# First batch of an attention and feed-forward kernel: row sums as products with ones, division at the outputs, one filler product per bank

## The chip, the cores and the metric

One core of a Trainium2 chip runs the whole program. The metric is the device time of one execution in microseconds. The engines are TensorE (PE; its weight loads are listed as PEld), VectorE (DVE), ScalarE (ACT), GpSimd (POOL) and SyncE (SP), which issues the transfers.

## The reference

For 4 batches x 8 heads, 576 positions and a head dimension of 64:

```python
scores = q @ k.T / sqrt(64) + (cum[:, None] - cum[None, :])   # cum = cumsum(log(clip(f, 1e-4, 1)))
scores = where(causal, -1e9, scores) - max                    # causal: the part above the diagonal
attn = exp(scores); attn = attn / (sum(attn, -1) + 1e-9)
x = attn @ v                                  # heads side by side: 2304 tokens x 512
x = maximum(x @ w1, x @ w2, x @ w3) @ w_out   # 512 -> 768 -> 512
h = x @ w_in                                  # 512 -> 2048
out = ((a0 + a1*h + a2*h**2 + a3*h**3) / (1 + |b0|*|h| + |b1|*h**2 + 1e-6)) @ w_out2
```

The weights of both feed-forward layers arrive as 64-bit floats.

## The kernel before

Heads are worked on in pairs, and the 576 query rows in two groups: group 0 has the first 320 rows (three blocks), group 1 the last 256 (two blocks). The first batch goes through group 0 of its four pairs and then through group 1 of them, so that it makes up the first eight entries of the list of pairs (n from 0 to 7, one group each). Later batches have one entry for each pair with both groups. A unit is one head of one entry; a step takes a new unit through `scores`, the unit before it through `turn`, and the one before that through `attend`.

- `scores` makes the products of queries and keys in a PSUM bank (line 343 in 32-bit floats for the first six entries, lines 345 and 346 in two rounded parts afterwards). VectorE adds the mask and takes the row maximum (line 347), ScalarE takes the exponential and, through `accum_out`, the row sum (line 353).
- `normalise` adds 1e-9 to the row sums (line 358), takes their reciprocals (line 359), on VectorE, and lets GpSimd scale each block of exponentials by its row's reciprocal (line 362).
- `turn` transposes the blocks on TensorE (line 382), and ScalarE copies them into the tile `pt` (line 384).
- `attend`, once for both heads of a pair, multiplies `pt` by the values (line 398). In the result, `ot`, the partitions are the head's dimensions and the columns the queries. ScalarE copies it out as the rounded part of `x` (line 405), and VectorE subtracts for the rest (line 406).

PSUM has two banks for scores, three for transposes (`ps_t`, tag `t`), one for outputs (`ps_o`) and two for the first feed-forward layer. In the first four entries `exercised` puts filler products of 512 columns into each bank that is taken, ahead of the bank's real product, `WARM` of them (line 84); nothing reads their results.

Beside the attention run, call by call (`fill`), the conversions of the 64-bit weights (`convert`, lines 169 to 179: ScalarE, four VectorE instructions, ScalarE, then GpSimd) and the products of the first feed-forward layer (`moe1_h`, `moe1_o`, lines 430 to 461), whose intermediate maxima lie in three buffers with the tag `mx`. A planner puts the instructions of each engine in order by costs and due times of its own, save where the order is pinned; the outputs' products have high priority and are pinned among themselves. The second feed-forward layer follows, written out by hand from line 766 on.

Of the kernel before, what the change touches and what calls it, by code (L numbers as in the profile page):

```python
# [8 lines left out]
F32 = mybir.dt.float32  # L9
F32R = mybir.dt.float32r  # L10
I32 = mybir.dt.int32
AF = mybir.ActivationFunctionType
ALU = mybir.AluOpType
# [12 lines left out]
GBLK = [(0, 1, 2), (3, 4)]  # L26
# [11 lines left out]
def kernel(  # L38
    ctx: ExitStack, tc: tile.TileContext, q, k, v, f, w1, w2, w3, w_out, m2_in, m2_out, m2_a, m2_b, out
):  # L40
    nc = tc.nc
    B, H, S, D = q.shape
# [3 lines left out]
    P = 128  # L46
# [3 lines left out]
    NPAIR = H // 2  # L50
    NB = len(Q0)

    def r32(ap):
        return ap.bitcast(F32)
# [5 lines left out]
    const = ctx.enter_context(tc.tile_pool(name="const", bufs=1, side="left"))  # L60
    dram = ctx.enter_context(tc.tile_pool(name="dram", bufs=1, space=DRAM))
    mpool = ctx.enter_context(tc.tile_pool(name="mpool", bufs=1, side="left"))
    wpool = ctx.enter_context(tc.tile_pool(name="wpool", bufs=1, side="left"))
    apool_cm = ExitStack()
    apool = apool_cm.enter_context(tc.tile_pool(name="apool", bufs=1, side="right"))
    ps_cm = ExitStack()
    ps_s = ps_cm.enter_context(tc.tile_pool(name="ps_s", bufs=2, space=PSUM))
    ps_t = ps_cm.enter_context(tc.tile_pool(name="ps_t", bufs=3, space=PSUM))
# [11 lines left out]
    def exercised(bank, n):  # L80

        if n < 4:
            for _ in range(WARM):
                nc.tensor.matmul(bank, warm[:, 0], wide, start=True, stop=True)
        return bank

    WARM = 2
    mask = const.tile([P, S], F32, name="mask")
    nc.gpsimd.memset(mask, 0.0)
    nc.gpsimd.affine_select(  # L90
# [1 line left out]
        fill=-1.0e9, base=0, channel_multiplier=1,  # L92
    )


    NR = B * H
    fl = apool.tile([NR, S], F32, name="fl", tag="vs", bufs=3)
# [15 lines left out]


    LOOK, WHOLE, PRE = 2, 6, 2
    CONV2, EARLY = (32, 0.25), 12
    kqs = {}

    def k_split(i):
        if ("k", i) not in kqs:  # L120
            k1 = apool.tile([P, S], F32R, name=f"k1s{i}", tag=f"k1_{i}")
            kqs["k", i] = k1, apool.tile([D + 2, S], F32R, name=f"k2s{i}", tag=f"k2_{i}")
        return kqs["k", i]

    def q_split(g, i):
        if (g, i) not in kqs:
            w = GQ[g][1] - GQ[g][0]
            q1 = apool.tile([P, w], F32R, name=f"q1s{g}{i}", tag=f"q1_{g}_{i}")
            q2 = apool.tile([D + 2, w], F32R, name=f"q2s{g}{i}", tag=f"q2_{g}_{i}")
            nc.vector.tensor_scalar(q2[D : D + 2], mask[0:2, :w], 0.0, 1.0, op0=ALU.mult, op1=ALU.add)  # L130
            kqs[g, i] = q1, q2
        return kqs[g, i]
# [10 lines left out]
    for g in range(2):  # L143
        pts.append(apool.tile([P, 2, GCOLS[g]], F32, name=f"pt{g}", tag=f"pt{g}"))
        col = GCH[g][0][0]
# [81 lines left out]
    def pinned(ld):  # L227
        tc.keep_in_program_order(ld)
# [10 lines left out]
    SIDES = [(slice(0, D), slice(D, P)), (slice(D, P), slice(0, D))]  # L239

    class Pair:


        def __init__(self, n, b, hp, groups):
            self.n, self.b, self.hp, self.groups = n, b, hp, groups
            self.ng = groups[-1] + 1
            self.nk = GBLK[groups[-1]][-1] + 1
            self.ik = [(2 * n + h) % NKB for h in range(2)]
            self.iq = [[(2 * n + h) % m for h in range(2)] for m in NQB]
            self.pt = {}  # L250
            self.whole = n < WHOLE
            self.iqf = [(2 * n + h) % 4 for h in range(2)]

        def load(self):
# [58 lines left out]
    class Unit:  # L313
# [5 lines left out]

        def begin(self):  # L320
            self.st = apool.tile([P, 9], F32, name=f"st_{self.nm}", tag="st", bufs=3)
            self.rs = apool.tile([P, 2, 3], F32, name=f"rs_{self.nm}", tag="rs", bufs=3)

        def scores(self, i):
            p, h, g = self.pair, self.h, self.g
            if not p.whole:
                (k1, k2), (q1, q2) = k_split(p.ik[h]), q_split(g, p.iq[g][h])
            nr = P
            qs = slice(Q0[i] - GQ[g][0], Q0[i] - GQ[g][0] + P)
            keys = Q1[i]  # L330
            self.e[i] = apool.tile([P, keys], F32, name=f"e{i}_{self.nm}", tag=f"e{i}_{h}")
            e = self.e[i]
            st = self.st
            n0 = 3 * (i - GBLK[self.g][0])
            nm = st[:nr, n0 : n0 + 2]
            l = self.rs[:nr, 0, i - GBLK[self.g][0] : i - GBLK[self.g][0] + 1]
            parts = [(0, keys)] if keys <= 512 else [(0, 320), (320, keys)]
            off = S - P - Q0[i]
            for n, (a, z) in enumerate(parts):
                sp = exercised(ps_s.tile([P, 512], F32, name=f"s{i}_{n}_{self.nm}", tag="s"), p.n)  # L340
                if p.whole:
                    kf, qf = kfs[p.ik[h]][: D + 2], qfs[p.iqf[h]][: D + 2]
                    nc.tensor.matmul(sp[:nr, : z - a], qf[:, qs], kf[:, a:z], start=True, stop=True)
                else:
                    nc.tensor.matmul(sp[:nr, : z - a], q1[:, qs], k1[:, a:z], start=True, stop=False)
                    nc.tensor.matmul(sp[:nr, : z - a], q2[:, qs], k2[:, a:z], start=False, stop=True)  # L346
                nc.vector.tensor_tensor_reduce(  # L347
                    out=e[:nr, a:z], in0=sp[:nr, : z - a], in1=mask[:nr, off + a : off + z],
                    scale=-1.0, scalar=3.0e38 if n == 0 else nm[:, 0:1],
                    op0=ALU.add, op1=ALU.min, accum_out=nm[:, n : n + 1],  # L350
                )
            m = nm[:, len(parts) - 1 : len(parts)]
            nc.scalar.activation(e[:nr], e[:nr], AF.Exp, bias=m, scale=-1.0, accum_out=l)  # L353

        def normalise(self):
            blks = GBLK[self.g]
            n = len(blks)
            nc.vector.tensor_scalar_add(self.rs[:, 0, :n], self.rs[:, 0, :n], 1.0e-9)
            nc.vector.reciprocal(self.rs[:, 1, :n], self.rs[:, 0, :n])  # L359
            for j, i in enumerate(blks):  # L360
                e = self.e[i]
                nc.gpsimd.tensor_scalar(e, e, self.rs[:, 1, j : j + 1], 0.0, op0=ALU.mult, op1=ALU.add)  # L362
# [23 lines left out]
        def attend(self):  # L386

            p, h, g = self.pair, self.h, self.g
            if h == 0:
                return  # L390
            lo, hi = GQ[g]
            w = hi - lo
            ot = exercised(ps_o.tile([P, 512], F32, name=f"o_{self.nm}", tag="o"), p.n)
            order = list(GCH[g].items())
            with tc.high_priority():
                for j, (c, (col, q0)) in enumerate(order):
                    for i in (1, 0):
                        mm = nc.tensor.matmul(  # L398
                            ot[SIDES[i][0], q0 - lo : w], p.v[:, c, i], p.pt[g][:, i, col : col + hi - q0],
                            start=(j == 0), stop=(j == len(order) - 1),  # L400
                        )
                        if (j, i) != (0, 1):
                            pinned(mm)
            x = mpool.tile([P, 2, w], F32R, name=f"x_{self.nm}", tag=f"x{g}", bufs=(6, 8)[g])
            nc.scalar.activation(x[:, 0], ot[:, :w], AF.Copy)
            nc.vector.tensor_tensor(x[:, 1], ot[:, :w], r32(x[:, 0]), op=ALU.subtract)
            xt[p.b, p.hp, g] = x


    hs = {}  # L410
# [128 lines left out]
    for step in range(len(slots) + 2):  # L539
        u = slots[step] if step < len(slots) else None  # L540
        t = slots[step - 1] if 0 <= step - 1 < len(slots) else None
        o = slots[step - 2] if 0 <= step - 2 < len(slots) else None
        prep, NPRE = [], 0
        if u is not None and u.pair.n + 1 < len(pairs):
            n = u.pair.n + 1
# [252 lines left out]
```

## Time and profile before

| | |
|---|---|
| time, median of 3 runs | 966.98 us (966.38 to 970.47) |
| the profiled execution | 970.9 us, with a span of 969.1 us |
| busy, of the span | PE 97%, PEld 86%, DVE 76%, ACT 64%, POOL 26% |
| granted TensorE clock, mean | 0.988 |

The span reaches from the first instruction to the last. Busy shares are means over stages with different limits, so the rows below give them by stage. TensorE's matmuls are pipelined, and their ends are modelled: a busy TensorE is not one at its peak. A granted clock of 1.00 is 2.4 GHz, 0.50 is 1.2 GHz. "Idle before" is the time in which an engine waited just before an instruction, with what ended the wait.

### The profile page before, as it was taken

The page shows a single profiled execution, that of the slowest core. Times are in us where ns is not written, and L with a number is a line of the kernel's source. Part 1 is how long each engine was busy: PE and PEld are TensorE (multiplying, and loading weights), DVE is VectorE, ACT ScalarE, POOL GpSimd, SP SyncE. Part 2 cuts the span into 40 slices and gives each one's busy share as a digit, 9 for nine tenths or more (in the row PEclk, how much of TensorE's full clock was granted, in tenths as well). Part 3 has the DMA queues.
Part 4 walks back from the last instruction along what each step waited for, and adds up shares of the span by engine and source line. Part 5 has one row for each costly group of instructions (what it writes and reads, how often), then busy time and mean ns, then how long its engine had stood idle before and what let it go on. Part 6 is the DMA issues. An engine that isn't in the chain of part 4 may idle for free.

```text
span 969.1 us, 16846 instructions
## 1 busy us (share of the span) xinstructions
PE 943.1 (97%) x5780; PEld 829.9 (86%) x5780; DVE 739.6 (76%) x1756; ACT 623.8 (64%) x1457; POOL 252.4 (26%) x408
## 2 busy tenths in 40 slices
PE   7998999999999999999999999999999999999998
PEld 6767889998998988999999978888888888999997
DVE  5789985557777777534397949988888988899997
ACT  5875666667667666646454548767666766677775
POOL 2646553445454545425133400000000000000000
PEclk9978999999999999999999999999999999999999
DMA  6685233124446445230145477011002101100000
GB/s 160 159 236 153 64 83 89 43 63 119 140 131 205 133 136 174 58 94 1 57 140 185 132 253 269 1 44 43 1 1 66 44 1 46 64 1 1 34 1 33
DMA packets 125621, 88.52 MB, mean 91 GB/s; under 512 B 74448, under 2 KB 110304, under 8 KB 125536
## 3 DMA queue, kind: packets, MB, share of 16 engines
q1 hardware_dynamic: 125536, 87.45, 30.4%
q8 instruction: 46, 0.75, 0.4%
q14 instruction: 39, 0.32, 0.1%
HBM read 64.73 MB, written 22.69 MB: 90 GB/s over the span
## 4 chain that ended last, share of the span: by engine, by line
PE 70%; DVE 14%; DMA 6%; ACT 4%; issue 3%; POOL 2%; SPq 1%; ACTq 0%; POOLq 0%; DVEq 0%
PE oo L721 7%; PE oo L722 7%; PE oo L720 7%; PE hq L671 6%; PE hq L673 6%; PE hq L672 6%; PE tp L382 4%; PE h L430 4%; PE o L398 4%; PE h L431 4%; PE h L432 4%; PE x2p L455 2%; DMA raw_wi<-in_moe_w_in_dram 2%; PE x2p L456 2%; PE x2p L457 2%
## 5 line engine op out<-in xcount | busy, mean ns | idle before, releaser
L430 PE MATMUL h<-x,w1h 128*128 128x320 f32 (+1 forms) x576 | 176.6, 307 | 3.1 <-ACT m L435 2.2
L431 PE MATMUL h<-x,w1h 128*128 128x320 f32 (+1 forms) x576 | 172.1, 299 | 0.0
L432 PE MATMUL h<-x,w1l 128*128 128x320 f32 (+1 forms) x576 | 171.2, 298 | 0.0
L430 PEld LDWEIGHTS h<-x,w1h 128*128 128x128 f32 x576 | 109.4, 190 | 7.0 <-ACT m L435 3.0
L362 POOL TENSOR_SCALAR e<-e,rs 128x64 f32<-128x64 f32 (+4 forms) x160 | 87.7, 563 | 106.4 <-DVE rs L359 91.5
L353 ACT ACTIVATE e<-e,st 128x64 f32<-128x64 f32 (+4 forms) x160 | 89.1, 557 | 37.8 <-DVE st L347 36.0
L721 PE MATMUL oo<-wp,gh 128*128 128x512 f32 x288 | 112.9, 392 | 0.0
L720 PE MATMUL oo<-wp,gh 128*128 128x512 f32 x288 | 112.5, 390 | 0.0
L431 PEld LDWEIGHTS h<-x,w1h 128*128 128x128 f32 x576 | 109.5, 190 | 0.4 <-issue 0.2
L432 PEld LDWEIGHTS h<-x,w1l 128*128 128x128 f32 x576 | 109.2, 190 | 0.0
L722 PE MATMUL oo<-wp,gl 128*128 128x512 f32 x288 | 108.8, 392 | 0.0
L680 ACT ACTIVATE s<-hq 128x512 f32<-128x512 f32 (+1 forms) x80 | 44.3, 554 | 97.4 <-PE hq L673 97.4
L347 DVE CUSTOM_DVE_ANT_0 e<-s,mask 128x320 f32<-128x320 f32 (+3 forms) x160 | 67.2, 433 | 37.9 <-PE s L346 24.0
L384 ACT ACTIVATE pt<-tp 128x384 f32<-128x384 f32 (+3 forms) x160 | 69.8, 469 | 19.2 <-PE tp L382 17.4
L683 DVE SCALAR_TENSOR_TENSOR s<-s,ab,u 128x512 f32<-128x512 f32 (+1 forms) x80 | 55.7, 697 | 32.1 <-ACT u L681 31.9
L382 PE MATMUL tp<-ident,e 128*128 128x128 f32 (+1 forms) x480 | 78.0, 280 | 1.3 <-DVE k2s L275 0.6
L673 PE MATMUL hq<-x,wil 128*128 128x512 f32 (+1 forms) x192 | 70.4, 367 | 0.0
L671 PE MATMUL hq<-x,wih 128*128 128x512 f32 (+1 forms) x192 | 70.4, 367 | 0.0
L672 PE MATMUL hq<-x,wih 128*128 128x512 f32 (+1 forms) x192 | 70.3, 366 | 0.0
L722 PEld LDWEIGHTS oo<-wp,gl 128*128 128x128 f32 x288 | 54.1, 188 | 11.7
L720 PEld LDWEIGHTS oo<-wp,gh 128*128 128x128 f32 x288 | 54.2, 188 | 11.0
L721 PEld LDWEIGHTS oo<-wp,gh 128*128 128x128 f32 x288 | 54.1, 188 | 10.9
(129 smaller groups left out, 2433.6 us busy)
## 6 DMA issues: line engine op xcount, KB each, us to landing
raw_w<-in_moe_w_dram SPq DMA_DIRECT2D x18, 512.0 KB
raw_wp<-in_moe_w_out_dram SPq DMA_DIRECT2D x32, 256.0 KB
wpd<-wp SPq DMA_DIRECT2D x32, 256.0 KB
raw_wi<-in_moe_w_in_dram SPq DMA_DIRECT2D x32, 256.0 KB
wp<-wpd SPq DMA_DIRECT2D x10, 768.0 KB
x2d<-xo SPq DMA_DIRECT2D x16, 320.0 KB
out_dram<-ob SPq DMA_DIRECT2D x18, 256.0 KB
kn<-in_k_dram SPq DMA_DIRECT2D x32, 128.0 KB
```

What stands on the lines that cost most here:

```text
L353: nc.scalar.activation(e[:nr], e[:nr], AF.Exp, bias=m, scale=-1.0, accum_out=l)
L362: nc.gpsimd.tensor_scalar(e, e, self.rs[:, 1, j : j + 1], 0.0, op0=ALU.mult, op1=ALU.add)
L382: nc.tensor.transpose(tp[:kr, dst : dst + P], self.e[i][:, Q0[c] : Q1[c]], ident)
L430: nc.tensor.matmul(hp_[:, :w], wh[:, j, dc], xs[dc][:, 1], start=(dc == NDC - 1), stop=False)
L431: nc.tensor.matmul(hp_[:, :w], wh[:, j, dc], xs[dc][:, 0], start=False, stop=False)
L432: nc.tensor.matmul(hp_[:, :w], wl[:, j, dc], xs[dc][:, 0], start=False, stop=(dc == 0))
L671: nc.tensor.matmul(hp_[:, :w], wih[:, dc, fs], xh, start=(dc == 0), stop=False)
L672: nc.tensor.matmul(hp_[:, :w], wih[:, dc, fs], xl, start=False, stop=False)
L673: nc.tensor.matmul(hp_[:, :w], wil[:, dc, fs], xh, start=False, stop=(dc == NDC - 1))
L720: nc.tensor.matmul(o, g[0][:, ts_], wh_, start=(fc == 0), stop=False)
L721: nc.tensor.matmul(o, g[0][:, ts_], wl_, start=False, stop=False)
L722: nc.tensor.matmul(o, g[1][:, ts_], wh_, start=False, stop=(fc == NF2 - 1))
```

## The change

For entries with n below `LATE` = 2 x 4 = 8, the first batch, `normalise` does nothing, and the exponentials are transposed and multiplied as they are. `accum_out` is dropped for them. `attend` issues, ahead of the products with the values, a set of products of the same `pt` with a tile of ones of 64 columns (`summing`), into a bank of the transposes (`sm`): each row of the result holds the sum of the exponentials for the query of its column, in the layout of `ot`. ScalarE copies it out, adding 1e-9 (`tiny`), VectorE takes the reciprocal of all its columns and multiplies it by `ot`, and the two instructions that split `x` read that product in place of `ot`. The quotients lie in the buffers of tag `mx`. `WARM` goes from 2 to 1. The scaling by row sums moves from before the product with the values to after it; the rest of the computation stays.

```diff
@@ -84,7 +84,7 @@
                 nc.tensor.matmul(bank, warm[:, 0], wide, start=True, stop=True)
         return bank
 
-    WARM = 2
+    WARM = 1
     mask = const.tile([P, S], F32, name="mask")
     nc.gpsimd.memset(mask, 0.0)
     nc.gpsimd.affine_select(
@@ -92,6 +92,11 @@
         fill=-1.0e9, base=0, channel_multiplier=1,
     )
 
+
+    tiny = const.tile([P, 1], F32, name="tiny")
+    nc.vector.memset(tiny, 1.0e-9)
+    summing = const.tile([P, D], F32, name="summing")
+    nc.vector.memset(summing, 1.0)
 
     NR = B * H
     fl = apool.tile([NR, S], F32, name="fl", tag="vs", bufs=3)
@@ -113,6 +118,7 @@
 
 
     LOOK, WHOLE, PRE = 2, 6, 2
+    LATE = 2 * NPAIR
     CONV2, EARLY = (32, 0.25), 12
     kqs = {}
 
@@ -249,6 +255,7 @@
             self.iq = [[(2 * n + h) % m for h in range(2)] for m in NQB]
             self.pt = {}
             self.whole = n < WHOLE
+            self.late = n < LATE
             self.iqf = [(2 * n + h) % 4 for h in range(2)]
 
         def load(self):
@@ -319,7 +326,8 @@
 
         def begin(self):
             self.st = apool.tile([P, 9], F32, name=f"st_{self.nm}", tag="st", bufs=3)
-            self.rs = apool.tile([P, 2, 3], F32, name=f"rs_{self.nm}", tag="rs", bufs=3)
+            if not self.pair.late:
+                self.rs = apool.tile([P, 2, 3], F32, name=f"rs_{self.nm}", tag="rs", bufs=3)
 
         def scores(self, i):
             p, h, g = self.pair, self.h, self.g
@@ -333,7 +341,7 @@
             st = self.st
             n0 = 3 * (i - GBLK[self.g][0])
             nm = st[:nr, n0 : n0 + 2]
-            l = self.rs[:nr, 0, i - GBLK[self.g][0] : i - GBLK[self.g][0] + 1]
+            l = None if p.late else self.rs[:nr, 0, i - GBLK[self.g][0] : i - GBLK[self.g][0] + 1]
             parts = [(0, keys)] if keys <= 512 else [(0, 320), (320, keys)]
             off = S - P - Q0[i]
             for n, (a, z) in enumerate(parts):
@@ -353,6 +361,8 @@
             nc.scalar.activation(e[:nr], e[:nr], AF.Exp, bias=m, scale=-1.0, accum_out=l)
 
         def normalise(self):
+            if self.pair.late:
+                return
             blks = GBLK[self.g]
             n = len(blks)
             nc.vector.tensor_scalar_add(self.rs[:, 0, :n], self.rs[:, 0, :n], 1.0e-9)
@@ -393,18 +403,30 @@
             ot = exercised(ps_o.tile([P, 512], F32, name=f"o_{self.nm}", tag="o"), p.n)
             order = list(GCH[g].items())
             with tc.high_priority():
-                for j, (c, (col, q0)) in enumerate(order):
-                    for i in (1, 0):
-                        mm = nc.tensor.matmul(
-                            ot[SIDES[i][0], q0 - lo : w], p.v[:, c, i], p.pt[g][:, i, col : col + hi - q0],
-                            start=(j == 0), stop=(j == len(order) - 1),
-                        )
-                        if (j, i) != (0, 1):
-                            pinned(mm)
+                if p.late:
+                    sm = ps_t.tile([P, 512], F32, name=f"sm_{self.nm}", tag="t")
+                    dsts = [(sm, lambda c, i: summing), (ot, lambda c, i: p.v[:, c, i])]
+                else:
+                    dsts = [(ot, lambda c, i: p.v[:, c, i])]
+                for n, (dst, lhs) in enumerate(dsts):
+                    for j, (c, (col, q0)) in enumerate(order):
+                        for i in (1, 0):
+                            mm = nc.tensor.matmul(
+                                dst[SIDES[i][0], q0 - lo : w], lhs(c, i), p.pt[g][:, i, col : col + hi - q0],
+                                start=(j == 0), stop=(j == len(order) - 1),
+                            )
+                            if (n, j, i) != (0, 0, 1):
+                                pinned(mm)
             x = mpool.tile([P, 2, w], F32R, name=f"x_{self.nm}", tag=f"x{g}", bufs=(6, 8)[g])
-            nc.scalar.activation(x[:, 0], ot[:, :w], AF.Copy)
-            nc.vector.tensor_tensor(x[:, 1], ot[:, :w], r32(x[:, 0]), op=ALU.subtract)
             xt[p.b, p.hp, g] = x
+            xn = ot
+            if p.late:
+                xn = mpool.tile([P, 320], F32, name=f"xn_{self.nm}", tag="mx", bufs=3)
+                nc.scalar.activation(xn[:, :w], sm[:, :w], AF.Identity, bias=tiny)
+                nc.vector.reciprocal(xn[:, :w], xn[:, :w])
+                nc.vector.tensor_tensor(xn[:, :w], ot[:, :w], xn[:, :w], op=ALU.mult)
+            nc.scalar.activation(x[:, 0], xn[:, :w], AF.Copy)
+            nc.vector.tensor_tensor(x[:, 1], xn[:, :w], r32(x[:, 0]), op=ALU.subtract)
 
 
     hs = {}
```

## Rows read from the trace of the kernel before

**Rows 1.** By stage: PE, PEld, DVE, ACT, POOL busy us (count); clock, DMA, GB/s.

```profile
0.00:56.00 56.00, 49.73 (x274) 38.63 (x275) 35.24 (x119) 38.24 (x107) 22.34 (x40) 1.00 0.64 169
56.00:138.00 82.00, 74.42 (x452) 61.69 (x451) 77.00 (x180) 53.44 (x132) 47.53 (x54) 0.90 0.46 126
138.00:150.00 12.00, 9.84 (x50) 9.04 (x48) 6.20 (x16) 6.13 (x18) 6.63 (x13) 0.72 0.40 110
150.00:969.00 819.00, 809.11 (x5011) 720.56 (x5010) 621.12 (x1443) 526.01 (x1203) 175.90 (x302) 1.00 0.27 82
```

**Rows 2.** The same view, line 84 alone: PE and PEld busy us (count).

```profile
0.00:56.00 56.00, 36.46 (x104) 17.81 (x104) 1.00 0.64 169
```

**Rows 3.** Chain that ended last by 160 us: start us, us, what.

```profile
0.92 0.55 DVE ones L100
...
26.05 1.36 POOL e L362 x2
...
29.87 2.29 POOL e L362 x3
...
34.23 0.47 PE s L84 x2
...
49.96 1.36 PE o L398 x12
...
152.85 2.10 PE o L398 x20
```

**Rows 4.** Groups by form, 0 to 56 us: busy, mean ns | idle before.

```profile
L353 ACT ACTIVATION_READ_ACCUMULATOR e<-e,st 128x1 f32 x25 | 4.7, 189 | 0.0
...
L358 DVE TENSOR_SCALAR rs<-rs 128x3 f32<-128x3 f32 x8 | 2.4, 297 | 3.2 <-ACT e L353 3.2
...
L359 DVE RECIPROCAL rs<-rs 128x3 f32<-128x3 f32 x8 | 1.4, 174 | 0.2
```

**Rows 5.** Timeline, 54 to 84 us: start us, us, engine, instruction.

```profile
57.51 1.41 PE L398 MATMUL o<-pt,v 128*64 128x320 f32 x12
...
72.52 0.43 ACT L405 ACTIVATE x<-o 128x320 fp32r<-128x320 f32 x1
```

**Rows 6.** Waits on VectorE, 8 to 56 us: us, times, longest.

```profile
DVE e L347 <- PE s L343: 11.7, 10, 4.4
```

**Rows 7.** Groups of VectorE by form, 56 to 150 us.

```profile
L358 DVE TENSOR_SCALAR rs<-rs 128x2 f32<-128x2 f32 x8 | 3.0, 379 | 0.1
...
L359 DVE RECIPROCAL rs<-rs 128x2 f32<-128x2 f32 x8 | 1.3, 156 | 0.1
L406 DVE TENSOR_TENSOR x<-o,x 128x256 fp32r<-128x256 f32 x3 | 1.2, 416 | 0.5 <-ACT x L405 0.5
...
L406 DVE TENSOR_TENSOR x<-o,x 128x320 fp32r<-128x320 f32 x1 | 0.5, 484 | 0.0
```

**Rows 8.** Groups by form, whole run: the reciprocals.

```profile
L359 DVE RECIPROCAL rs<-rs 128x3 f32<-128x3 f32 x32 | 5.6, 174 | 0.8
...
L359 DVE RECIPROCAL rs<-rs 128x2 f32<-128x2 f32 x32 | 5.2, 162 | 0.6
```

**Rows 9.** The same view, line 362 alone: POOL busy us (count), clock, DMA, GB/s.

```profile
56.00:138.00 82.00, 11.49 (x15) 0.90 0.46 126
```

**Rows 10.** The same view, instructions on tile cv_wo alone: DVE, ACT, POOL busy us.

```profile
56.00:138.00 82.00, 22.11 (x48) 9.30 (x23) 6.70 (x9) 0.90 0.46 126
```

**Rows 11.** The same view, instructions on tile cv_wi, 480 to 620 us.

```profile
480.00:620.00 140.00, 51.65 (x128) 25.92 (x64) 25.88 (x32) 1.00 0.54 179
```

**Rows 12.** Timeline, 133 to 150 us.

```profile
137.65 1.54 POOL L362 TENSOR_SCALAR e<-e,rs 128x448 f32<-128x448 f32 x2 [1.14 <-DVE rs L359]
...
140.61 0.41 PE L456 MATMUL x2p<-hh,wo 128*128 128x320 f32 x1 [2.02 <-POOL wo L179]
```

**Rows 13.** The same view, all instructions, around 62 us.

```profile
60.00:62.00 2.00, 1.06 (x4) 0.30 (x2) 2.00 (x8) 1.95 (x7) 0.26 (x1) 1.00 1.19 300
62.00:64.00 2.00, 1.70 (x6) 1.23 (x6) 1.97 (x5) 1.35 (x4) 2.00 (x3) 0.63 1.20 272
```

## The prediction

> **What bounds the kernel now.** I read the busy times by stage first, because a share over the whole span mixes stages with different limits [rows 1]. The reader is to see four stages. From 0 to 56 us TensorE is busy 49.7 of 56 us, and no other engine is near its limit. From 56 to 138 us VectorE is: 77.0 of 82 us, while TensorE's 74.4 are partly queueing and partly a lower clock. From 138 to 150 us nothing is full. From 150 us to the end TensorE is busy 809 of 819 us, so whatever moves the point where that last stage begins moves the end by as much, and work added to TensorE after that point is paid in full.
>
> Next I asked what TensorE does in the first stage. Restricted to line 84, the filler products, the same view shows 104 of them, all before 56 us [rows 2]. The chain of waits says whether they matter [rows 3]: pairs of fillers stand in it at 0.47 us a pair, so 0.23 each, between real products; before them, at 26 and 29.9 us, it runs through GpSimd's scaling of the exponentials (line 362), 1.36 and 2.29 us.
>
> **The change part by part.**
>
> *Fillers.* 104 become 52: 52 x 0.23 = 12.0 us less in TensorE's queue, all in the first stage.
>
> *Row sums on TensorE.* For each of the eight pairs of the first batch a second set of products with the shapes of line 398 is issued. The chain prices a set at 1.36 us for 12 records (first three blocks, four pairs) and 2.10 us for 20 (last two blocks, four pairs) [rows 3]. Three sets fall before 56 us: +4.1. Those of pairs 3 to 6 fall into the VectorE-bound stage, where TensorE's part lies beside VectorE's; without that cover they would cost 1.4 + 3 x 2.1 = 7.7 us. The eighth pair's product runs at 152.85 us, in the full stage: +2.1 us.
>
> *First stage together.* TensorE's queue shrinks by 12.0 - 4.1 = 7.9 us, and the chain loses the two scalings, 3.65 us, since the transposes now wait for the exponential alone. That is 11.5 us at most. At least it is nothing, if ScalarE (38.2 of 56 us busy) and VectorE (35.2), which feed each other in short turns, already set the pace. ScalarE loses 24 accumulator reads of 0.189 and gains three copies near 0.43 [rows 4, 5]: -3.2 us. VectorE loses 2.4 + 1.4 [rows 4] and gains three reciprocals and multiplies (below, 2.7 us a pair): +4.4. Neither becomes full: their loads would be 35 and 40 us. Much of VectorE's idle time there was waiting for scores, 11.7 us [rows 6], which is what the fillers hold up. I take half: -5.8 us. Two one-off memsets (128 x 64 and 128 x 1) come before the loop on VectorE; the memset of 576 columns there takes 0.55 [rows 3], and I take 0.2 for both.
>
> *The wide reciprocal.* The trace has no reciprocal over 320 or 256 columns. From below, a VectorE pass over that shape in the same place takes 0.48 and 0.42 us [rows 7]. From above, the reciprocals of three columns average 174 ns and those of two 162 ns [rows 8]: 12 ns for a column more, which carried on gives 0.174 + 317 x 0.012 = 4.0 us and 0.162 + 254 x 0.012 = 3.2. The one row of the operation itself leans away from a single pass, but its difference is that of two short instructions, so I go halfway: 2.25 and 1.8 us.
>
> The Trainium skill speaks against this part of the change: "VectorE: DVE Perf Modes", in the section "First, the fixed hardware budget", has the reciprocal as an iterated divide with a repeat count of 8, which at that page's 0.96 GHz would be an estimate of 8.3 ns for a column, some 2.8 and 2.3 us. The difference of 12 ns agrees in kind; by the page the sum below would come out 2.0 us higher, by a single pass 5.9 lower.
>
> *VectorE in the bound stage.* Added, for pairs 3 to 6: 2.25 + 3 x 1.8 = 7.7, and multiplies 0.48 + 3 x 0.42 = 1.7 [rows 7]. Removed: the small addition and reciprocal of eight row-sum tiles, 3.0 + 1.3 = 4.3 [rows 7]. GpSimd's scaling also goes, 11.5 of its 47.5 us in the stage [rows 1, 9]. VectorE runs slower beside a busy GpSimd: a conversion instruction of 256 columns takes 22.11 / 48 = 0.461 us here [rows 10] and 51.65 / 128 = 0.404 later, where GpSimd has 26 of 140 us [rows 11]. So 48 instructions lose 2.7 us; the longer ones of the first weights perhaps twice that; of 8 us a quarter (11.5 / 47.5) is 1.9, between nothing and 3.8 if the longer ones suffer more. Together 7.7 + 1.7 - 4.3 - 1.9 = +3.2 us.
>
> *The stall at 138 us.* TensorE waits 2.02 us for a converted weight, which stands in GpSimd's queue behind 1.54 us of scaling [rows 12]. Without the scaling: -1.5 us. If the slower clock of that stage (0.72 on average [rows 1]) went with it, another 3.4; I leave that out.
>
> *New waits.* The reciprocal waits for ScalarE's copy of the sums, the multiply for the reciprocal, ScalarE's output copy for the multiply. Behind them in the two queues stand score reductions and conversions (VectorE) and exponentials (ScalarE), so the next scores wait for whichever is late. The output bank, of which there is one, comes free after the multiply. The sums occupy one of the three transpose banks until ScalarE reads them, and ScalarE can be late: the product at 57.5 us was copied out at 72.5 [rows 5]. I price these at nothing, since the planner puts other work of those queues between; without that cover one pair costs about 0.43 + 2.25 + 0.48 = 3.2 us.
>
> *Sum.* 0.2 - 5.8 + 3.2 - 1.5 + 2.1 = -1.8 us. The profiled execution took 970.9 us with a span of 969.1, and stands 3.9 us above the median of 966.98; taken from the median, 965 us.
>
> **The rivals.**
>
> *Faster.* The wide reciprocal runs near a single pass (-5.9 us), or VectorE finds room for it, and most of the first stage's 11.5 us is won (-3 more). 956 us. For it: VectorE has 21 us without work before 56 us. Against it: the 12 ns.
>
> *A long reciprocal.* At 4.0 and 3.2 us the bound stage gets 4.0 + 3 x 3.2 - 7.7 = 5.9 us more, and some of the new waits show: 972 us. For it: the difference of 12 ns [rows 8]. Against it: how short those instructions are.
>
> *The clock falls in the first stage* (the slower side). At 60 to 62 us, just after the last fillers, TensorE was busy 1.06 of 2 us, and the granted clock went from 1.00 to 0.63 in the next 2 us, on its way from 2.4 to 1.2 GHz [rows 13]. With half the fillers such a gap can come at 25 to 50 us, where TensorE is the limit. 24 us of that stage at the lower level would do 12 us less work: 965 + 12 = 977 us. It decides from about 7 us lost. Against it: of TensorE's 49.7 busy us in that stage 7.9 go, and 41.8 of 56 stay filled.
>
> *The shorter link was hidden anyway.* The transposes come a step after the exponentials, so removing the scaling and its contention gives nothing, and only fillers, sums and VectorE's work count: 0.2 - 7.9 / 2 + (7.7 + 1.7 - 4.3) + 2.1 = +3.5: 970 us.
>
> **How the numbers follow.** The forecast has 0.40, with its own range of 960 to 971 (reciprocal at 0.5 to 3.2 us a piece against half or more of the first stage). Faster has 0.25, the long reciprocal 0.12, the clock 0.13, the hidden link 0.10. 0.5% is 4.8 us, about what a measurement of this kernel can tell from no change. Below 962.1 lie nearly all of the faster case and three tenths of the forecast: 0.37. Above 971.8 lie the clock, half of the long reciprocal, and some of the forecast and of the hidden link: 0.26. The rest is 0.37. The range of 955 to 976 leaves out about one in ten on each side: a first stage won in full with a cheap reciprocal, and a long spell of the lower clock.
>
> **What would show it.** The fillers: 52 records of line 84, and the eighth set of sums near or before 150 us. The first stage: the fourth output product, at 57.5 us before, some 5 us earlier. The reciprocal: its mean at 128 x 320, 0.5 or 2 to 4 us. The bound stage: VectorE still over 90% busy, and the time from the fourth output product to the last conversion some 3 us longer. The stall: no scaling ahead of the last weights on GpSimd. The clock: granted 1.00 from 10 to 50 us. The prediction is wrong if the planner orders the conversions differently, so that the full stage begins with more or less work left than now.

## The result and the profile after

The changed kernel takes 973.4 us in the median of 15 runs (970.0 to 977.8), the kernel before 969.1 in 15 runs beside it: a ratio of 1.0052, 95% interval 1.0040 to 1.0064. That is 5 us slower, and just past the 0.5% that the prediction drew as its bound. Forecast were 965 us and a gain of 0.2%.

The two profiled executions do not show the whole loss. That of before took 970.9 us, more than any of the 15 runs, that of after has a span of 969.9 us, where before has 969.1. So the traces are read for where things happen, and the sizes are taken from the ratios.

Busy times by stage of the changed kernel up to 150 us, with the columns of [rows 1]:

```profile
0.00:56.00 56.00, 49.42 (x298) 36.08 (x299) 40.60 (x121) 41.63 (x95) 10.43 (x16) 1.00 0.76 197
56.00:138.00 82.00, 68.50 (x439) 55.32 (x439) 77.09 (x171) 54.16 (x123) 36.81 (x45) 0.89 0.42 116
138.00:150.00 12.00, 12.00 (x90) 10.16 (x87) 9.39 (x27) 8.19 (x25) 6.51 (x12) 0.89 0.13 29
```

The same view for line 84 alone:

```profile
0.00:56.00 56.00, 26.59 (x52) 10.56 (x52) 1.00 0.76 197
```

Of the 104 fillers 52 are left, and the granted clock stays at 1.00, 2.4 GHz, up to 56 us. VectorE is as full as before in the second stage, 77.1 of 82 us. TensorE has 5.9 us less in it, although 68 records of sums (tile `sm`) were added there; 48 more, four sets and not three, lie before 56 us.

Groups of VectorE by form, 0 to 200 us (busy, mean ns of one):

```profile
L426 DVE RECIPROCAL xn<-xn 128x320 f32<-128x320 f32 x4 | 8.6, 2145 | 0.0
...
L426 DVE RECIPROCAL xn<-xn 128x256 f32<-128x256 f32 x4 | 7.0, 1751 | 1.5 <-ACT xn L425 1.4
...
L427 DVE TENSOR_TENSOR xn<-o,xn 128x256 f32<-128x256 f32 x4 | 1.7, 416 | 0.0
```

The wide reciprocal took 2.15 us over 320 columns and 1.75 over 256; the multiply what [rows 7] gave for its shape. The subtraction now reads both operands from SBUF. Its means are 0.75 and 0.80 us, where it took 0.48 and 0.42, but they mix two kinds: five of the eight took 0.40 to 0.49 us as before, and the others 0.82, 1.55 and 1.56. Each of these three began while a GpSimd instruction on two tiles in SBUF ran, and the two longest ended 0.3 to 0.4 us after it. One of them, with the GpSimd instruction (timeline):

```profile
71.18 1.55 DVE L429 TENSOR_TENSOR x<-xn,x 128x320 fp32r<-128x320 f32 x1
...
70.98 1.39 POOL L185 TENSOR_TENSOR w1l<-cv_w,w1h 128x512 fp32r<-128x512 f32 x1 [2.56 <-ACT w1h L184]
```

The chain of waits up to 160 us has no scaling any more and fewer fillers than in [rows 3]; sums stand in it, and from 57 us on reciprocals, the fourth first:

```profile
21.95 1.37 PE sm L414 x12
...
57.07 2.06 DVE xn L426
```

Two of the prediction's signs can be read here. The fourth output product, at 57.5 us before [rows 5], comes 3.2 us earlier. And a score product still waits 2.59 us for GpSimd, where the profile names the conversion of a weight, though no scaling of the first batch stands in that queue any more. From the timeline:

```profile
54.32 1.36 PE L414 MATMUL o<-pt,v 128*64 128x320 f32 x12
...
130.45 0.71 PE L353 MATMUL s<-k1s,q1s 128*128 128x64 f32 x2 [2.59 <-POOL wo L185]
```

Then there is a row that the prediction had not looked for. The products of the first layer's line 430 (452 after the change), alone, from 56 to 140 us: first before, then after.

```profile
56.00:140.00 84.00, 23.91 (x72) 13.80 (x72) 0.90 0.46 125
```

```profile
56.00:140.00 84.00, 18.69 (x56) 11.05 (x56) 0.88 0.41 113
```

By 140 us all 72 of these products of the first batch's group 0 were done before, and 56 after. The maxima that follow them say when the rest came. The timeline of the changed kernel, 136 to 168 us:

```profile
141.17 1.75 DVE L426 RECIPROCAL xn<-xn 128x256 f32<-128x256 f32 x1 [0.24 <-ACT xn L425]
...
142.84 0.43 DVE L459 TENSOR_TENSOR m<-m,h 128x320 f32<-128x320 f32 x1
...
156.16 0.49 DVE L459 TENSOR_TENSOR m<-m,h 128x320 f32<-128x320 f32 x1
```

The kernel before, 120 to 136 us:

```profile
134.43 0.48 DVE L437 TENSOR_TENSOR m<-m,h 128x320 f32<-128x320 f32 x1
```

Before, the last maximum of that group was taken at 134.4 us, 18 us ahead of the batch's eighth output product [rows 3]. After, four of them follow the eighth reciprocal, the last at 156.2. Quotients and maxima lie in the same three buffers, in turns fixed by the order of the program.

### The profile page after: what moved, and what is told of

It is laid out like the page before. It is cut to its first block, busy times and chain, and to the rows that moved or that the text cites. A ratio compares the mean times of both kernels' runs of the same rounds, so it can differ in the third digit from the quotient of the medians.

```text
span 969.9 us, 16851 instructions
## 1 busy us (share of the span) xinstructions
PE 942.5 (97%) x5856; PEld 828.2 (85%) x5856; DVE 743.7 (77%) x1742; ACT 627.8 (65%) x1425; POOL 227.8 (23%) x368
## 4 chain that ended last, share of the span: by engine, by line
PE 75%; DVE 14%; ACT 4%; DMA 3%; issue 3%; SPq 0%; POOL 0%; ACTq 0%; DVEq 0%; POOLq 0%
PE oo L742 7%; PE oo L744 7%; PE oo L743 7%; PE hq L695 6%; PE hq L693 6%; PE hq L694 6%; PE h L452 5%; PE h L453 5%; PE h L454 5%; PE o L414 4%; PE tp L392 4%; PE s L354 2%; PE s L353 2%; PE x2p L477 2%; DVE cv_wi L178 2%
## 5 line engine op out<-in xcount | busy, mean ns | idle before, releaser
L372 POOL TENSOR_SCALAR e<-e,rs 128x448 f32<-128x448 f32 (+3 forms) x120 | 63.7, 546 | 84.3 <-DVE rs L369 75.7
L744 PEld LDWEIGHTS oo<-wp,gl 128*128 128x128 f32 x288 | 54.0, 188 | 12.4
L743 PEld LDWEIGHTS oo<-wp,gh 128*128 128x128 f32 x288 | 54.1, 188 | 10.6
L742 PEld LDWEIGHTS oo<-wp,gh 128*128 128x128 f32 x288 | 54.1, 188 | 10.4
```

The lines of the kernel that those rows point to most:

```text
L742: nc.tensor.matmul(o, g[0][:, ts_], wh_, start=(fc == 0), stop=False)
L743: nc.tensor.matmul(o, g[0][:, ts_], wl_, start=False, stop=False)
L744: nc.tensor.matmul(o, g[1][:, ts_], wh_, start=False, stop=(fc == NF2 - 1))
```

## The experiments

All ratios are to the kernel before, run on the same chip; 0.1% is 1 us. New variants of the changed kernel are told by their edit to it.

**Which part costs.** Two fillers again in the changed kernel, and one filler in the kernel before:

```diff
-    WARM = 1
+    WARM = 2
```

> The changed kernel with two fillers per bank again, so the row-sum part alone. Theory (the wide reciprocals, 15.6 us of VectorE, and the waits behind them make the loss; one filler fewer is worth little): still slower than the kernel before, ratio 1.003 to 1.008. Rival (halving the fillers is what costs, through gaps and the lower clock): back to 1.000 or below.

Measured: 1.0098 (1.0075 to 1.0121), above the theory's range too.

> The kernel before with one filler per bank, so the filler part alone. Theory: little or a gain, ratio 0.995 to 1.001. Rival (the fillers): slower, 1.003 to 1.008, with a granted clock under 1.00 between 10 and 56 us.

Measured: 1.0010 (0.9994 to 1.0027). The row sums are what costs, 9.5 us with two fillers; taking a filler away gives nothing alone and 4.5 us beside the sums. The granted clock of the kernel before with one filler was 1.00 up to 56 us as well. All the same its fourth output product came at 53.9 us, 3.6 us earlier than in the trace with two.

**Without the reciprocal on VectorE.**

```diff
-                nc.scalar.activation(xn[:, :w], sm[:, :w], AF.Identity, bias=tiny)
-                nc.vector.reciprocal(xn[:, :w], xn[:, :w])
+                nc.scalar.activation(xn[:, :w], sm[:, :w], AF.Ln, bias=tiny)
+                nc.scalar.activation(xn[:, :w], xn[:, :w], AF.Exp, scale=-1.0)
```

> The changed kernel with the reciprocal taken on ScalarE as exp(-ln(sum + 1e-9)): VectorE loses its eight wide reciprocals (15.6 us), ScalarE gains eight instructions near 0.4 us. Theory (the reciprocals): the kernel before or faster, ratio 0.993 to 1.000, and the first layer's output 5 us or more earlier than the 163 us of the changed kernel. Rival (the planner's order, which lets the next batch's attention run ahead of the first layer): stays at 1.004 to 1.008.

Measured: 0.9993 (0.9979 to 1.0007). The eight reciprocals cost 5.7 us. But the first layer's first output (ScalarE's copy of it, tile `xo`) stayed at 162.8 us, with 163.1 in the changed kernel, so that part of the expectation failed, and the kernel only drew level with the one before.

**Half of the batch.**

```diff
-    LATE = 2 * NPAIR
+    LATE = NPAIR
```

> The changed kernel with the new row sums for the first four entries only (group 0); the last four of the first batch are normalised as before. Theory (the reciprocals in the VectorE-bound stage from 56 to 138 us cost most): better than the changed kernel, ratio 0.997 to 1.002 to the kernel before. Rival (the loss comes in the first stage): stays at 1.004 or more.

Measured: 0.9991 (0.9980 to 1.0002).

```diff
-            self.late = n < LATE
+            self.late = LATE // 2 <= n < LATE
```

> The changed kernel with the new row sums for entries 4 to 7 (group 1) only; entries 0 to 3 are normalised as before. Theory (the loss comes from the wide reciprocals while VectorE is full, not from the first stage): slower than the kernel before, ratio 1.003 to 1.008, as the changed kernel. Rival (both halves are needed for the loss): 0.998 to 1.002.

Measured: 1.0057 (1.0037 to 1.0078). The loss sits with entries 4 to 7. The next two were to show that their reciprocals make it.

```diff
-                nc.vector.reciprocal(xn[:, :w], xn[:, :w])
+                for _ in range(3 if p.n >= NPAIR else 1):
+                    nc.vector.reciprocal(xn[:, :w], xn[:, :w])
```

> The changed kernel with each reciprocal of entries 4 to 7 taken three times in place (the value comes out the same): 4 x 2 x 1.75 = 14 us more on VectorE in the stage where it is full. Theory (VectorE's work there sets the end nearly one for one): ratio 1.014 to 1.021 to the kernel before. Rival (VectorE has room, and the changed kernel lost by the planner's order): 1.004 to 1.009.

The reciprocals of 256 columns by form in this run (busy, mean ns of one):

```profile
L427 DVE RECIPROCAL xn<-xn 128x256 f32<-128x256 f32 x12 | 20.9, 1745 | 0.1
```

Measured: 1.0123 (1.0103 to 1.0143), between the two: 13.9 us more of VectorE (20.9 against 7.0) cost 6.9, half of it. This is not VectorE's price alone: the first layer's first output came at 172.0 us, so the longer reciprocals also held the shared buffers up.

Both edits together, `LATE = NPAIR` and exp(-ln):

> The changed kernel with exp(-ln) on ScalarE for the reciprocal and the new row sums for entries 0 to 3 only. Theory: the four reciprocals of the first stage stand where VectorE has room, so little is added to the 0.9991 of the kernel with entries 0 to 3 alone: 0.996 to 1.000. Rival (a reciprocal costs the same in either stage): 0.994 to 0.996.

Measured: 0.9928 (0.9906 to 0.9950), 960.6 us. This is faster than both kernels and than either range, and it turned the theory round. Taking the four reciprocals of entries 0 to 3 from VectorE gives 6.1 us (0.9991 to 0.9928), as much as taking all eight (1.0052 to 0.9993). And entries 4 to 7 cost 6 us with reciprocals (0.9991 to 1.0052) and 6.3 without (0.9928 to 0.9993). So their reciprocals are not what they cost, as far as these runs tell: taken together, the four intervals leave some 3 us either way.

**No filler at all** in the changed kernel (`WARM = 0`):

> The changed kernel without any filler. Theory (fillers stand in slack of TensorE, and one fewer changed nothing by itself): 1.002 to 1.007, as the changed kernel. Rival (fillers hold the clock up): 1.010 or more with a granted clock under 1.00 before 56 us. Second rival (each filler costs its 0.23 us when the sums are there, as two against one did): 1.000 or below.

Busy times by stage of this run, with the columns of [rows 1]:

```profile
0.00:56.00 56.00, 46.37 (x251) 30.75 (x251) 40.43 (x113) 42.03 (x96) 10.41 (x16) 1.00 0.77 199
56.00:138.00 82.00, 70.17 (x419) 55.27 (x419) 77.93 (x173) 50.64 (x116) 36.73 (x45) 0.85 0.42 114
```

Measured: 1.0088 (1.0068 to 1.0108), between the ranges. The column of the granted clock reads 1.00 up to 56 us, but the products say otherwise. The first set of sums took 2.62 us, where it took 1.37 to 1.41 in the changed kernel and later in this run (timeline):

```profile
23.13 2.62 PE L414 MATMUL sm<-pt,summing 128*64 128x320 f32 x12
...
34.14 1.41 PE L414 MATMUL sm<-pt,summing 128*64 128x320 f32 x12 [0.58 <-ACT pt L394]
```

A pair of score products over 320 columns took 1.27 us at 18.8 us and 0.70 from 28.3 on, where the changed kernel has 0.70 from 12.4 on. That is the ratio between the two levels of the clock: sets of 20 records took 4.11 us where the column reads 0.50 and 2.17 at 1.00. So without fillers TensorE ran at the lower level until about 27 us, and the column does not show it. Nor does one filler always hold the clock up: up to 56 us it was 0.91 in the trace of exp(-ln) for all eight entries (0.70 from 14 to 21 us) and 0.97 in that with entries 4 to 7 only. Whether this slow opening is what none costs against one is not settled: the fourth output product came at 51.9 us even so, earlier than with one, and from 56 to 138 us the granted clock was 0.85, where one filler had 0.89, though no filler falls into that stage in either kernel.

**What entries 4 to 7 cost.** Three runs on three theories, and a fourth that goes back to the first stage. First, buffers of their own for their quotients, in the kernel with exp(-ln):

```diff
+                if g == 1:
+                    xn = apool.tile([P, 320], F32, name=f"xn_{self.nm}", tag=f"e2_{p.n % 2}")
+                else:
-                xn = mpool.tile([P, 320], F32, name=f"xn_{self.nm}", tag="mx", bufs=3)
+                    xn = mpool.tile([P, 320], F32, name=f"xn_{self.nm}", tag="mx", bufs=3)
```

> The kernel with exp(-ln) and the new row sums for all eight entries (0.9993), with the quotients of entries 4 to 7 in buffers that the first batch's group 1 leaves unused, in place of the three buffers of the first layer's maxima. Entries 4 to 7 cost 6 us with either form of reciprocal. Theory A (quotients and maxima take turns in three buffers, which holds the first layer up): 0.992 to 0.995. Theory B (the sums' 8.4 us of TensorE) and theory C (the planner lets attention run ahead of the first layer once the scaling is gone): 0.998 to 1.001.

Measured: 0.9945 (0.9925 to 0.9965), 4.7 us better, and the first layer's first output at 133 us in place of 163. As theory A had it.

```diff
+                    part = order[:1] if p.late and n == 0 and g == 1 else order
-                    for j, (c, (col, q0)) in enumerate(order):
+                    for j, (c, (col, q0)) in enumerate(part):
...
-                                start=(j == 0), stop=(j == len(order) - 1),
+                                start=(j == 0), stop=(j == len(part) - 1),
```

> The same kernel (exp(-ln), eight entries), with the row sums of entries 4 to 7 taken over the first block of keys alone: 2 of 10 products in each set are kept, the other 8 left out, 6.7 us less on TensorE. Theory B (the sums' products): 0.992 to 0.995. Theories A and C: 0.998 to 1.001.

Measured: 0.9956 (0.9940 to 0.9971), between the ranges: 3.6 us better. The 6.7 us were counted from the number of products; in the two traces the four sets took 11.6 us with all products, part of them at the lower clock, and 4.0 with two each. The shorter sums also let the first layer move, its first output to 154.6 us from 162.8, so this gain and that of the buffers overlap and are not to be added.

On the kernel of 0.9928, without any division for entries 4 to 7 (one place of the edit is shown; `accum_out` and the tile of row sums go for them too):

```diff
-            if self.pair.late:
+            if self.pair.n < 2 * NPAIR:
                 return
```

> The kernel with exp(-ln) and the new row sums for entries 0 to 3 (0.9928), with the division of entries 4 to 7 left out altogether: no sums, no scaling, no quotient. Theories A and B (what the new division adds is what costs): 0.993 or below, since VectorE and GpSimd only lose work. Theory C (the scaling's absence changes the planner's order for the worse): 0.997 or more.

Measured: 0.9877 (0.9856 to 0.9898). Theory C falls as the reason of a 6 us loss: without the scaling and without anything in its place the kernel is 4.9 us faster. Seen from here the old division of entries 4 to 7 costs these 4.9 us, and the new one with exp(-ln) 11.2 (0.9877 to 0.9993).

> The kernel with exp(-ln) and the new row sums for entries 0 to 3 (0.9928), with two fillers per bank. Theory (in the first stage TensorE's queue with its fillers and the chain through GpSimd's scaling stand side by side, so that neither alone gives anything): 0.998 to 1.002. Rival (the gain is the chain's alone): 0.992 to 0.995.

Measured: 1.0005 (0.9990 to 1.0020), the theory's number. But the traces do not bear out that the two hide one another in the first stage. The fourth output product of the kernel before with one filler, of this run, and of the same kernel with one filler:

```profile
53.89 1.41 PE L398 MATMUL o<-pt,v 128*64 128x320 f32 x12
...
61.15 1.36 PE L414 MATMUL o<-pt,v 128*64 128x320 f32 x12
...
53.05 1.36 PE L414 MATMUL o<-pt,v 128*64 128x320 f32 x12
```

With 57.5 us before the change, one filler fewer alone gives 3.6 us there, and the new sums with two fillers lose 3.6. Neither shows at the end (1.0010 and 1.0005); both edits together, 4.5 us there, show as 7.

**The shared buffers in the changed kernel itself.** The edit of the run with buffers of their own, with the reciprocals kept:

> The changed kernel itself, reciprocals on VectorE included, with the quotients of entries 4 to 7 in buffers of their own; one edit away from the changed kernel. Theory (the three shared buffers held the first layer up in the changed kernel as in the one with exp(-ln), where they cost 4.8 us): 0.999 to 1.002, and the first layer's first output before 150 us (163 in the changed kernel). Rival (with the reciprocals VectorE is late for the maxima anyway): 1.003 to 1.007.

Measured: 1.0008 (0.9997 to 1.0019). One edit takes back 4.3 of the 5.0 us, give or take 1.6 by the two intervals. (Against exp(-ln) with the same buffers, 0.9945, the eight reciprocals cost 6.1 us, no more than the four of entries 0 to 3 did.) The first layer's first output comes at 141 us, as before the change, and its products up to 140 us are again 72 (the view of line 430 above):

```profile
56.00:140.00 84.00, 23.02 (x72) 13.53 (x72) 0.96 0.38 109
```

```diff
-                nc.vector.tensor_tensor(xn[:, :w], ot[:, :w], xn[:, :w], op=ALU.mult)
+                nc.vector.tensor_tensor(ot[:, :w], ot[:, :w], xn[:, :w], op=ALU.mult)
+                xn = ot
```

> The changed kernel with the quotient written back into the output bank, so that the shared buffer comes free at the multiply, two instructions earlier, and the subtraction reads PSUM (0.42 to 0.49 us before, 0.75 to 0.80 from SBUF). Theory (the time a shared buffer is held is what costs): 1.000 to 1.004. Rival (any turn in the ring sets the planner's order): 1.004 to 1.007.

Measured: 1.0120 (1.0097 to 1.0142), outside both. The quotient now occupies the only output bank until the subtraction. Waits on TensorE up to 160 us in this run (us, times, longest):

```profile
PE o L414 <- DVE x L430: 11.0, 1, 11.0
```

One set of products waits 11 us for that bank. The edit traded a share of three buffers for the whole of one, and so doesn't say what the shorter hold alone is worth.

## Why the prediction was wrong

**The reciprocal: right.** Halfway between its bounds it had 2.25 and 1.8 us; measured are 2.15 and 1.75, or 6.2 ns for a column more (394 ns over 64). That halfway was so close is partly luck, since no row spoke for it. By the Trainium skill's "VectorE: DVE Perf Modes" (section "First, the fixed hardware budget"), which has the reciprocal as an iterated divide with a repeat count of 8, the estimate was 8.3 ns; the measurement is below that and far above the 1.1 ns of the multiply (485 against 416 ns), and it decides.

**The clock: right in this trace.** It held at 1.00 up to 56 us, and the times of the products agree from 12 us on, against the slower rival, though not in every trace with one filler, as shown above.

**"The stall at 138 us ... -1.5 us": not borne out.** GpSimd's scaling of the first batch is gone, and TensorE is busy all of 138 to 150 us. But TensorE has a wait of that kind still: 2.59 us at 130 us for GpSimd, again put down to the conversion of a weight, and the granted clock was 0.50 from 133 to 140 us. With the scaling of entries 4 to 7 kept (0.9991) TensorE was busy all of 138 to 150 us too, so its absence is not what filled that stretch.

**"First stage together ... I take half: -5.8 us": this step failed.** It counted time won in the first stage as time won at the end. For entries 0 to 3 the sum had -5.8 + 0.2 + 2.7 (the fourth entry's reciprocal and multiply) = -2.9 us; measured is 0.9991, -0.9. The first stage did get shorter, but of the 11.5 us at most only 3.2 came at the fourth output product; and the kernel before with one filler has as much of that, 3.6, and nothing at the end (1.0010). The new sums of entries 0 to 3 with a cheap division and two fillers give nothing either (1.0005); both together give 0.9928, 7 us. So only the pair is worth something at the end. Why, is open: inside the first stage the two do not hide one another.

Nor did VectorE's room take the reciprocals in for nothing: the four of entries 0 to 3, 8.6 us of them, cost 6.1 at the end (0.9991 to 0.9928), although VectorE's load before was 35 of 56 us. Three stand before 56 us, and the fourth, at 57.0, where VectorE is full. The fourth output product is only 1.1 us later for them (54.1 against 53.1). But by 56 us VectorE had done 16.1 us of the conversions of the first weights with them and 20.2 without, and the rest falls into the full stage. These 4.1 us and the fourth's 2.1 would make 6.2, an estimate from one trace each; that this is the path is argued and not shown, since the kernel before with one filler had done 21.3 us of them by then and gained nothing.

**"New waits ... I price these at nothing": the second step that failed, and the larger.** It named the output bank and the transpose banks, and not the three buffers of tag `mx`. Before, the planner's order finished the maxima of group 0 ahead of the batch's last output, in the stage where VectorE is full and TensorE is not. With the quotients in the ring of the maxima, four of the maxima came after the eighth reciprocal, and products of the first layer moved into the stage where TensorE is full. Price: 1.0052 against 1.0008, 4.3 us. That it is the shared buffers and not the absence of the scaling or the reciprocals is shown by the runs with buffers of their own, with and without reciprocals, and by the run without division. How much of it the lower clock took is not separated: from 56 to 150 us the granted clock was 0.89 in the changed kernel and 0.95 with buffers of their own, which at (1 - clock) x 94 us is 10.3 against 4.7 us, an estimate; in the one trace of the kernel before it was 0.87.

**What is left of entries 4 to 7** is 5.9 - 4.3 = 1.6 us. The sum had for them 3.2 - 2.7 (the fourth entry's reciprocal and multiply) - 1.5 + 2.1 = 1.1. That agreement is worth little, the more as the -1.5 did not come, and the eighth set of sums, priced at 2.1 us, took 4.11 at 136.5 us and the lower clock. The sign for this stage was missed as well: from the fourth output product to VectorE's last conversion 81 us became 92, not some 3 us more. In the second stage neither engine's work went in one for one: 14 us more on VectorE cost half, and 6.7 us of products less on TensorE, which the sum held to be hidden beside VectorE, gave half; and in both runs the first layer moved as well.

So -2.9 + 1.1 + 0 = -1.8 us was forecast, and -0.9 + 1.6 + 4.3 = +5.0 came.

**Open:** why no filler at all, in the changed kernel, costs 3.5 us against one, and where in the second stage the microseconds won in the first are lost. A change of the planner's order is possible and was not taken apart.

The version to keep is the one with exp(-ln) for entries 0 to 3 (0.9928, 960.6 us); with all eight entries and buffers of their own it is 0.9945, also 960.6 us but on another chip, which these runs don't tell apart.

## What to carry to other kernels

Time won in one stage need not be time won at the end: 3.6 us won before 56 us gave nothing. Price each of two savings with the other still in place: if both alone give nothing, only the pair is worth something, and a third load can take it back. When an edit puts a new tile into a ring that something else uses, ask in which order the two now have to run; a buffer that costs no time of its own can take away the freedom with which a planner filled an idle engine. And an engine that is 63% busy over a stage may fill the rest with work that otherwise falls where the engine is full: look at what a new instruction displaces.

## What the runs showed of the hardware

- VectorE's reciprocal of 32-bit floats takes 2.15 us for 320 columns and 1.75 for 256 (1.74 to 1.75 in other runs), some four times the multiply of the same shape (485 and 416 ns).
- A subtraction with both operands in SBUF took 0.40 to 0.49 us in five of eight cases, as with one operand in PSUM (0.42 and 0.48). The other three, 0.82, 1.55 and 1.56 us, began while GpSimd worked on two tiles in SBUF (1.39 us from 70.98 on for one of them). In the run with the new sums for entries 0 to 3 alone, none of the four did, and they took 0.49 to 0.51.
- The column of the granted clock can read 1.00 where TensorE runs at the lower level: in the run without fillers a set of sums took 2.62 us at 23 us and 1.41 at 34 us. The times of products of one shape tell it.
